# Emitting the routing and experts' stage of a retention and mixture-of-experts kernel by a model of the engines

## The chip, the cores and the metric

The kernel runs on one core of one Trainium2 chip. The metric is the device time of one execution in microseconds (us). A core has five engines that each work through their own list of instructions in order: TensorE (PE, matmuls), VectorE (DVE), ScalarE (ACT), GpSimd (POOL) and SyncE (SP, which here issues DMA transfers). An instruction starts when the one ahead of it on its engine has left and the semaphores that it waits for are there. So the order in which the kernel's author emits instructions decides what an engine does next, even when something further down its list could start already.

## The reference

Three steps follow each other: a retention (a decaying linear attention), a dense layer with a squared ReLU, and a mixture of eight experts in which each expert takes exactly 384 tokens. What matters here is the last one:

```python
def _moe2_ref(x, w_gate, w1, w2):          # x is 3072 x 512, E = 8, F = 1024
    cap = N // E                            # 384
    logits = x @ w_gate
    order = np.argsort(-logits.flatten())
    for idx in order:                       # the best pair first
        tok, e = int(idx) // E, int(idx) % E
        if assigned[tok] >= 0 or counts[e] >= cap:
            continue
        assigned[tok] = e
        counts[e] += 1
    for e in range(E):
        mask = assigned == e
        h = np.maximum(x[mask] @ w1[e], 0.0)
        out[mask] = h @ w2[e]
```

Matmuls must hold more than a 16-bit mantissa: each is made of three products of a high and a low part (high by high, high by low, low by high).

## The kernel before

The retention and the first layer fill the first 617 us. The stage that the change touches comes after them. It goes expert by expert, in the order in which experts become full, with these pieces:

- **Last block of the first layer** (`x_last`, L708): three matmuls for each of 16 slices f and four token groups c, emitted as the list `order`. Each finished group is copied by ACT (L712) and stored to the table `x2d` in DRAM (L714).
- **Search** (`search`, with `begin`): finds which tokens the next expert takes. Six rounds each of a count on PE (24 small matmuls, L831), a comparison of the counts on DVE (`sat`, L876), and new digits and comparisons on DVE (`cmp`, L823). Then come `TOT` (L909), a copy of it by ACT (`tots`, L911), and the slot matmuls (L923, L924), which this text calls the SLOT. After the SLOT, `begin` prepares the next search on DVE, with an expansion `EH` on ACT (L799, four pieces).
- **Index** (`index`): DVE makes the one-hot tables `ob`, `oa`, `pay` (L948 to L956); PE matmuls them (L962); `ixs` and L970 follow, and DVE ends with `idx` (L976).
- **Fetch** (`fetch`): POOL gathers the 384 token rows from `x2d` by `idx` in three indirect DMAs (L985). PE transposes them (`turn`, L1002). ACT makes the high part `gh` (L1024) and DVE the low part `gl` (L998).
- **Weights**: SP loads each slice f of an expert (512 KB, `eraw`, L1050) into four buffers. ACT makes the high part `h` (L1057) and DVE the low part `l` (L1066).
- **Expert** (`mlp`): for each of eight slices f, 12 matmuls into a PSUM bank (`eh_unit`, L1085; the bank alternates between 2 and 3). ACT takes the ReLU's high part `hh` (L1088) and DVE the low part `hl` (L1094), which reads the bank. Two slices later nine matmuls go into the output banks (`ey_unit`, L1106). At an expert's end `yo` is copied by ACT (L1110) and scattered by POOL (L1112).

The order comes from a weave. PE's main work is a list of units with a cost each. The sides (searches, indexes, weights, fetches) are generators that yield due times, written out by hand as tables:

```python
    SY=(4300, 3500, 2900, 450, 2600, 1200),
    IY=(600, 4600, 800),
    FE=(6500, 2800, 600),
```

`Weave.unit` adds the cost of a unit to a clock and steps each side whose time has come. What a side emits between two yields goes out in one piece on whichever engines it uses. The high and low parts of weights are emitted by `prep`, tied to places in the expert's units, in the fetch and in `fill`. Until the first tokens of expert 0 are there, PE runs 40 matmuls of ones (L1172), 28 of them as units and 4 after each of three groups of transposes.

## Time and profile before

| | us |
|---|---|
| median of three runs | 1043.21 (1043.13 to 1046.05) |
| the profiled execution | 1043.38 |
| its span, from the first to the last instruction | 1041.5 |
| PE busy | 989.6 (95%) |
| DVE busy | 714.3 (69%) |
| ACT busy | 452.8 (43%) |
| POOL busy | 77.7 (7%) |
| mean granted share of TensorE's clock | 0.991 |

The span is 1.9 us shorter than the profiled execution, and that execution is 0.2 us above the median. A busy share is a mean over the whole kernel; a stretch, or the waits of one engine, tells where time is lost. A row of a timeline gives the start and the duration of an instruction (or of several alike, with xN); in brackets stands how long its engine had been idle before, and what ended that. Matmuls overlap, so their starts tell the pace better than their durations.

### The profile page before, as it was taken

Reading aid. Unit: us, or ns where it says so; the run is one execution under the profiler, and the core shown is the slowest. Engines: PE = TensorE matmul, PEld = TensorE weight load, DVE = VectorE, ACT = ScalarE, POOL = GpSimd, SP = SyncE. Lnnn points to the kernel's source line nnn. Section 1 sums busy time; section 2 is a strip of 40 time slices with the busy share of each in tenths; the row PEclk is TensorE's granted clock in tenths of the full one; section 3 lists DMA queues with packets and bytes.
Section 4 is the critical chain, followed back from the end, with each engine's and each line's share of the span. In section 5 each row is a group of like instructions: output and inputs, shape, how many; then the busy total and the mean of one; then the engine's idle time right before and its main releaser. Section 6 shows DMA issues by size and latency. Waiting matters only on the chain.

```text
span 1041.5 us, 18741 instructions
## 1 busy us (share of the span) xinstructions
PE 989.6 (95%) x7356; PEld 861.5 (83%) x7356; DVE 714.3 (69%) x1778; ACT 452.8 (43%) x887; POOL 77.7 (7%) x100
## 2 busy tenths in 40 slices
PE   6899999999999999999999999799898889999997
PEld 5789998789899999899888777678787778788996
DVE  4799994587887787887763524666876768765531
ACT  2467665444344444344434551413434343533531
POOL 3200002000000000000000000011111020220211
PEclk9999999999999999999999999999999999999999
DMA  8533344332212120312130000513252433525620
GB/s 280 183 110 141 121 162 146 121 101 68 93 39 84 29 93 24 98 33 91 22 104 30 1 1 2 183 53 126 96 173 76 148 122 112 172 90 174 192 81 30
DMA packets 35031, 104.30 MB, mean 100 GB/s; under 512 B 4736, under 2 KB 5376, under 8 KB 34944
## 3 DMA queue, kind: packets, MB, share of 16 engines
q1 hardware_dynamic: 30384, 89.49, 26.6%
q0 software_dynamic: 3840, 12.59, 3.5%
q8 instruction: 57, 0.93, 0.4%
q10 hardware_dynamic: 720, 1.05, 0.3%
q14 instruction: 30, 0.25, 0.1%
HBM read 90.52 MB, written 12.58 MB: 99 GB/s over the span
## 4 chain that ended last, share of the span: by engine, by line
PE 68%; DVE 15%; issue 7%; DMA 5%; ACT 3%; POOL 2%; SPq 0%; POOLq 0%; DVEq 0%; ACTq 0%
PE b L419 22%; PE b L452 17%; PE b L1106 7%; PE b L1085 7%; DMA big<-x2d,idx 3%; PE b L708 2%; PE b L353 2%; PE b L326 2%; PE b L363 2%; PE b L831 2%; DVE raw L265 1%; POOL big L985 1%; DVE l L1066 1%; DVE raw L253 1%; DVE rl L442 1%
## 5 line engine op out<-in xcount | busy, mean ns | idle before, releaser
L475 DVE SCALAR_TENSOR_TENSOR scr<-tmp,wg 128x512 bf16<-128x512 f32 x288 | 198.0, 687 | 8.7 <-ACT tmp L462 3.8
L419 PE MATMUL b<-xh,l 128*128 128x256 f32 (+1 forms) x640 | 188.3, 294 | 3.4 <-DVE l L269 3.4
L419 PE MATMUL b<-xh,h 128*128 128x256 f32 (+1 forms) x640 | 188.8, 295 | 0.8 <-ACT xh L373 0.8
L419 PE MATMUL b<-xl,h 128*128 128x256 f32 (+1 forms) x640 | 188.1, 294 | 0.3 <-DVE xl L374 0.3
L426 ACT ACTIVATE r<-b 128x256 f32<-128x256 f32 x160 | 61.2, 383 | 192.6 <-PE b L419 184.3
L419 PEld LDWEIGHTS b<-xh,h 128*128 128x128 f32 x640 | 122.1, 191 | 11.0 <-ACT xh L373 1.3
L452 PE MATMUL b<-h,rh 128*128 128x512 f32 x320 | 129.3, 404 | 0.0
L419 PEld LDWEIGHTS b<-xl,h 128*128 128x128 f32 x640 | 122.0, 191 | 7.9 <-DVE xl L374 0.5
L419 PEld LDWEIGHTS b<-xh,l 128*128 128x128 f32 x640 | 122.1, 191 | 6.5 <-DVE l L269 3.8
L452 PE MATMUL b<-l,rh 128*128 128x512 f32 x320 | 126.5, 395 | 0.0
L452 PE MATMUL b<-h,rl 128*128 128x512 f32 x320 | 125.6, 392 | 0.8 <-DVE rl L442 0.8
L442 DVE TENSOR_TENSOR rl<-r,rh 128x256 fp32r<-128x256 f32 x160 | 68.5, 429 | 45.4 <-ACT rh L435 45.3
L1085 PE MATMUL b<-gh,h 128*128 128x384 f32 x256 | 91.0, 356 | 8.4 <-DVE hl L1094 8.4
L1066 DVE TENSOR_TENSOR l<-eraw,h 128x1024 fp32r<-128x1024 f32 x64 | 77.9, 1219 | 23.4 <-ACT h L1057 22.8
L1085 PE MATMUL b<-gh,l 128*128 128x384 f32 x256 | 86.7, 339 | 0.0
L1085 PE MATMUL b<-gl,h 128*128 128x384 f32 x256 | 86.5, 338 | 0.0
L1106 PE MATMUL b<-h,hl 128*128 128x512 f32 x192 | 76.8, 400 | 4.0 <-DVE hl L1094 4.0
L434 ACT ACTIVATE r<-r 128x256 f32<-128x256 f32 (+1 forms) x176 | 77.0, 438 | 5.6
L1106 PE MATMUL b<-h,hh 128*128 128x512 f32 x192 | 79.1, 412 | 0.0
L1106 PE MATMUL b<-l,hh 128*128 128x512 f32 x192 | 76.0, 396 | 0.0
L1088 ACT ACTIVATE hh<-b 128x384 fp32r<-128x384 f32 x64 | 31.3, 488 | 102.7 <-PE b L1085 96.4
L452 PEld LDWEIGHTS b<-h,rl 128*128 128x128 f32 x320 | 60.4, 189 | 15.2 <-DVE rl L442 1.5
(235 smaller groups left out, 1754.9 us busy)
## 6 DMA issues: line engine op xcount, KB each, us to landing
eraw<-in_w_dram SPq DMA_DIRECT2D x64, 512.0 KB, 3.6
q<-in_qkv_dram SPq DMA_DIRECT2D x36, 512.0 KB, 4.3
raw<-in_w_dram SPq DMA_DIRECT2D x32, 512.0 KB, 4.3
x2d<-tmp SPq DMA_DIRECT2D x20, 256.0 KB, 2.0
qdec<-in_dec_dram SPq DMA_DIRECT2D x18, 256.0 KB, 2.8
wg<-in_wgT_dram SPq DMA_DIRECT2D x4, 512.0 KB
x2d<-tmp ACTq DMA_DIRECT2D x3, 256.0 KB
first0h<-in_qkv_dram SPq DMA_DIRECT2D x2, 256.0 KB, 4.7
```

The source lines that it names most:

```text
L326: PE.matmul(ps[s][:, p * 128:(p + 1) * 128], kT[ss, p, :], qT[ss, p, :], start=(p == 0), stop=True, skip_group_check=True)
L353: PE.matmul(py[ss, p * 128:(p + 1) * 128], vt[:, p, ss], am[:, s, p], start=(p == 0), stop=(c == 0), skip_group_check=True)
L419: PE.matmul(ph, a[:, ks], b[..., kc, :], start=(kc == 0 and n == 0), stop=(kc == KC - 1 and n == 2))
L426: ACT.activation(r, ph, AF.Relu)
L434: ACT.activation(r, r, AF.Square)
L442: DVE.tensor_tensor(rl, r, rh.bitcast(F32), op=OP.subtract)
L452: PE.matmul(X2[blk][t], a[:, ts], b, start=(f == 0 and i == 0), stop=(f == NF - 1 and i == 2))
L475: DVE.scalar_tensor_tensor(scr, x, 1.0, WG[e], op0=OP.mult, op1=OP.mult, accum_out=of[:, e:e + 1])
L1066: DVE.tensor_tensor(lo, raw, hi.bitcast(F32), op=OP.subtract)
L1085: PE.matmul(PH[0], a[:, ks], b[:, kc, :], start=(kc == 0 and n == 0), stop=(kc == KC - 1 and n == 2))
L1088: ACT.activation(hh, PH[0], AF.Relu)
L1106: PE.matmul(Y[i, t], a[:, ts], b, start=(f == 0 and j == 0), stop=(f == NF2 - 1 and j == 2))
```

## The change

The weave of the last stage is replaced by a planner. Each generator now yields, ahead of each small group of instructions, the engine, a duration in ns, the names of the results that the group needs and the name of the one that it gives. `Plan` keeps one clock for each engine. Over and over it picks the stream whose next group could begin first by this model (plus a small bias for a stream), and lets that stream emit. The tables `SY`, `IY`, `FE`, `FZ` and `BG` are gone. Index and search are cut into finer groups. Weights go part by part, as three streams of their own: loads, high parts, low parts. The copies of the last block, the parts `hh`/`hl` and `gh`/`gl`, and the outputs become streams of their own that begin when their input is there by the model. No operation of the computation is added or taken away; of the matmuls of ones 30 are left.

```diff
+class Plan:
+    def begin(self, r):
+        eng, ns, needs, gives, lat, keep = r
+        if any(d not in self.T for d in needs):
+            return None
+        return max([self.clk[eng]] + [self.T[d] + keep for d in needs])
+
+    def run(self):
+        while self.streams:
+            best = None
+            for s in list(self.streams):
...
+                t = self.begin(s[1])
+                if t is not None and (best is None or t + s[2] < best[0]):
+                    best = (t + s[2], t, s)
...
+            _, t, s = best
+            eng, ns, _, gives, lat, _ = s[1]
+            self.clk[eng] = t + ns
+            if gives is not None:
+                self.T[gives] = t + ns + lat
...
+            self.advance(s)
+
+LAT = {"PE": 190.0, "ACT": 50.0, "DVE": 50.0, "POOL": 2600.0, "Q": 2500.0}
...
-    SY=(4300, 3500, 2900, 450, 2600, 1200),
-    IY=(600, 4600, 800),
...
+    KEEP=600.0,
...
-            ACT.dma_start(x2d[row:row + 128, ns], u[:, ns])
+    def x_row(c, half):
+        yield act(620 if half is None else 410, ("x", NF - 1, c, half), gives=("u", c, half))
...
-        yield SY[4]
-
+        yield pe(100, ("stb", i), *(() if last else (("ca", i),)), gives=("tot", i), keep=KEEP)
         tot = bank(6)
         PE.matmul(tot[:, 0:128], stb, ones_b, start=True, stop=True)
+        yield act(290, ("tot", i), gives=("tots", i))
...
         for t in range(GT):
+            yield op("POOL", 950 if t else 1760, ("idx", i), "x2d", gives=("xg", i, t))
...
+                yield pe(340, *(("xg", i, t) for t in range(GT)), need, gives=("T", i, kc), keep=KEEP)
...
+    def e_load():
+        for n in range(E * NF2):
...
+            yield op("Q", 1600, ("ei", i), *((("lo", n - 4),) if n > 3 else ()), gives=("raw", n))
...
+    def e_high():
...
+            yield act(1060, ("raw", n), old, gives=("hi", n))
...
+    def e_low():
...
+            yield dve(1220, ("hi", n), gives=("lo", n))
...
-    def eh_out(i, f):
-        hh, ph = HH[i, f]
-        hl = ff.tile([128, CAP], F32R, name="hl", bufs=3)
+    def eh_out(i, f, ph):
+        yield act(500, ("ph", i, f), gives=("hh", i, f))
+        hh = FF[0].tile([128, CAP], F32R, name="hh", bufs=3)
+        ACT.activation(hh, ph, AF.Relu)
+        yield dve(560, ("hh", i, f), gives=("hl", i, f))
...
+    def mains():
...
+                        yield pe(525, *needs, gives=("ph", i, f) if kc == KC - 1 else None)
+                        eh_unit(i, f, kc)
+                    plan.add(eh_out(i, f, PH[0]), -200)
...
-    for _ in range(28):
-        wv.unit(220, lambda: ones(1))
```

**Place 1: ACT, at the end of the first search** (last block of the first layer; `b_7119` and `b_7105` are the bank of `TOT`, `h_7114` and `h_7143` the first weight part). Before:

```order
L1057 ACTIVATE h_7114<-eraw 128x1024
L911 ACTIVATE tots<-b_7119 128x128
L712 ACTIVATE tmp<-b_6670,sb 128x512
L714 DMA x2d<-tmp 128x512
L1057 ACTIVATE h_7167<-eraw 128x1024
```

After:

```order
L986 ACTIVATE tots<-b_7105 128x128
L1127 ACTIVATE h_7143<-eraw 128x1024
L779 ACTIVATE tmp<-b_6670,sb 128x512
L781 DMA x2d<-tmp 128x512
L1127 ACTIVATE h_7166<-eraw 128x1024
```

The copy `tots` has moved from behind the first weight part to ahead of it.

**Place 2: DVE, behind the SLOT of the fourth search** (`hl` is the low part of a slice; `b_8982` and `b_8993` are the bank of slice f=1 of expert 2, counted from 0, and `b_8960` that of f=0). Before:

```order
L823 TENSOR_TENSOR cmp<-d,jt 128x1512
L952 TENSOR_TENSOR oa<-lowp,c_6307 128x384
L955 TENSOR_SCALAR pay<-oa,c_6307 128x24x16
L956 TENSOR_TENSOR pay<-oa,c_6307 128x24x16
L1066 TENSOR_TENSOR l_8976<-eraw,h_8975 128x1024
L1094 SCALAR_TENSOR_TENSOR hl<-b_8982,hh 128x384
```

After:

```order
L892 TENSOR_TENSOR cmp<-d,jt 128x1512
L1017 SCALAR_TENSOR_TENSOR sl<-s_8927 128x24
L1020 TENSOR_SCALAR lowp<-sl 128x24
L1021 TENSOR_SCALAR sl<-sl 128x24
L1024 TENSOR_TENSOR ob<-sl,c_6307 128x576
L1162 SCALAR_TENSOR_TENSOR hl<-b_8960,hh 128x384
L1028 TENSOR_TENSOR oa<-lowp,c_6307 128x384
L1032 TENSOR_SCALAR pay<-oa,c_6307 128x24x16
L1033 TENSOR_TENSOR pay<-oa,c_6307 128x24x16
L1162 SCALAR_TENSOR_TENSOR hl<-b_8993,hh 128x384
```

The first `hl` now stands ahead of `oa` and `pay`, the second right behind them, and no weight part stands between.

**Place 3: PE, around the same SLOT** (L1085 writes the bank of slice f=1 of expert 2; L1174 writes the output bank `b_8390` of expert 1, from its last two slices). Before:

```order
L1085 MATMUL b_8982<-gh,h_8722 128x384
L1085 MATMUL b_8982<-gl,h_8722 128x384
L1085 MATMUL b_8982<-gh,l_8723 128x384
L923 LDWEIGHTS strict
L923 MATMUL b_8986<-stb_6325,strict 128x48
L924 LDWEIGHTS tots
L924 MATMUL b_8986<-strict,tots 128x48
```

After:

```order
L1174 MATMUL b_8390<-h_8237,hl 128x512
L998 LDWEIGHTS strict
L998 MATMUL b_8914<-stb_6325,strict 128x48
L999 LDWEIGHTS tots
L999 MATMUL b_8914<-strict,tots 128x48
L1174 MATMUL b_8390<-h_8326,hh 128x512
```

The SLOT has moved from between the slices of the next expert back into the output matmuls of the current one. Behind it there now stand 15 output matmuls and 24 matmuls of slices before slice f=2 wants the bank that f=0 used; before, 21 matmuls of slices and 9 output matmuls stood between it and the first matmul of f=3, which wants the bank of f=1.

## Rows read from the trace of the kernel before

**Rows 1.** Four stretches: length, busy us (instructions) of PE, PEld, DVE, ACT, POOL; PEclk, DMA.

```profile
617.00:678.60 61.60, 55.72 (x432) 44.99 (x431) 32.81 (x115) 18.21 (x26) 0.00 (x0) 0.97 0.24 84
678.60:691.80 13.20, 11.80 (x124) 6.96 (x120) 6.19 (x25) 1.67 (x4) 3.18 (x3) 1.00 0.26 72
691.80:966.60 274.80, 252.34 (x2054) 215.63 (x2053) 193.91 (x602) 106.31 (x170) 39.28 (x52) 0.99 0.38 124
966.60:1035.00 68.40, 68.18 (x349) 61.53 (x347) 26.22 (x33) 26.05 (x40) 8.11 (x15) 1.00 0.30 101
```

**Rows 2.** What PE waited for, 617 to 1042 us: total us, times, longest.

```profile
PE b L1085 <- DVE hl L1094: 8.4, 3, 3.5
PE b L962 <- DVE pay L956: 4.9, 4, 1.6
PE b L1002 <- DMA big<-x2d,idx: 4.8, 8, 1.4
PE b L923 <- ACT tots L911: 4.1, 1, 4.1
PE b L1106 <- DVE hl L1094: 4.0, 4, 2.0
PE b L909 <- DVE sat L904: 1.4, 1, 1.4
```

**Rows 3.** Timeline at the first SLOT: start, us, engine, line, operation [idle before].

```profile
659.82 1.06 ACT L1057 ACTIVATE h<-eraw 128x1024 fp32r<-128x1024 f32 x1 [7.89 <-DMA eraw<-in_w_dram]
660.79 0.26 ACT L911 ACTIVATE tots<-b 128x128 bf16<-128x128 f32 x1
661.10 0.20 PE L923 MATMUL b<-stb,strict 128*128 128x48 bf16 x1 [4.15 <-ACT tots L911]
```

**Rows 4.** The three stretches of the stage with a lower granted clock, as in rows 1.

```profile
661.20:664.40 3.20, 3.20 (x10) 2.54 (x10) 2.79 (x11) 1.17 (x2) 0.00 (x0) 0.56 0.62 252
797.00:801.00 4.00, 4.00 (x36) 3.39 (x35) 1.49 (x4) 0.91 (x2) 0.00 (x0) 0.57 0.72 219
831.00:835.50 4.50, 4.50 (x16) 3.11 (x15) 0.00 (x0) 1.38 (x4) 2.15 (x4) 0.62 0.17 62
```

**Rows 5.** Timeline of PE and DVE behind the SLOT of 787 us.

```profile
787.15 0.43 PE L1085 MATMUL b<-gh,h 128*128 128x384 f32 x1
787.76 0.20 DVE L926 SCALAR_TENSOR_TENSOR s<-b,stb 128x48 f32<-128x48 f32 x1
790.92 0.39 PE L1106 MATMUL b<-h,hh 128*128 128x512 f32 x1
792.77 0.40 PE L1106 MATMUL b<-h,hl 128*128 128x512 f32 x1
793.65 0.55 DVE L952 TENSOR_TENSOR oa<-lowp,c 128x384 f16<-128x384 int32 x1
794.47 0.55 DVE L956 TENSOR_TENSOR pay<-oa,c 128x384 f16<-128x384 f16 x1
794.94 1.22 DVE L1066 TENSOR_TENSOR l<-eraw,h 128x1024 fp32r<-128x1024 f32 x1
796.07 0.55 DVE L1094 SCALAR_TENSOR_TENSOR hl<-b,hh 128x384 fp32r<-128x384 f32 x1
796.68 0.44 PE L1085 MATMUL b<-gh,h 128*128 128x384 f32 x1 [3.52 <-DVE hl L1094]
```

**Rows 6.** Timeline of two gathers: `idx`, POOL's third gather, the transpose that waited.

```profile
804.06 0.18 DVE L976 TENSOR_REDUCE idx<-rm 128x3 int32<-128x24 f32 x1
807.80 0.95 POOL L985 DMA_INDIRECT big<-x2d,idx  x1 [0.30 <-issue]
811.56 0.33 PE L1002 MATMUL b<-ident,big 128*128 128x128 f32 x1 [0.72 <-DMA big<-x2d,idx]
...
932.25 0.18 DVE L976 TENSOR_REDUCE idx<-rm 128x3 int32<-128x24 f32 x1
935.93 1.64 POOL L985 DMA_INDIRECT big<-x2d,idx  x1 [0.30 <-issue]
942.47 0.33 PE L1002 MATMUL b<-ident,big 128*128 128x128 f32 x1 [0.79 <-DMA big<-x2d,idx]
```

## What the change does to the time

> **What bounds the kernel now.** I read the views in this order: the stretches of the last stage, then the waits of PE, then the timeline at the longest waits. PE is the bound: in the four stretches from 617 to 1035 us it is busy for all but 29.9 us [rows 1]. Of that, 5.9 us lie before 678.6 (last block and first search), 1.4 between 678.6 and 691.8 (the wait for the first tokens, mostly covered by matmuls of ones), 22.5 while searches run beside experts 0 to 5, and 0.2 behind 966.6, where no search is left. So the end runs at PE's own pace, and nothing is to be had there. DVE, busy 194 of 275 us in the third stretch, is no bound by its total; what counts is how its list is ordered.
>
> The waits name the culprits [rows 2]. 12.4 us (8.4 + 4.0) are for `hl`; 4.9 for `pay`; 4.8 for gathered tokens; 4.1 for `tots`; 1.4 ahead of `TOT`, listed under `sat`. Two timelines show why. At the first SLOT, ACT holds `tots` behind a weight part whose DMA had not landed: ACT idles 7.89 us, then works on the weight from 659.82, and only at 660.79 copies `tots`, so PE stands 4.15 us [rows 3]. At 787 us DVE goes from the SLOT's result (787.76) through the next search's start and the whole index to the end of `pay` (795.02), then through a weight's low part, and `hl` ends at 796.62; PE, which needs its bank, had stood 3.52 us [rows 5]. The granted clock fell to half three times in the stage [rows 4]. The first two falls stand right behind these two waits.
>
> **The change part by part.** The arithmetic stays; only the order moves. Removing a wait is worth its length as long as nothing else is late then. All sums start from the profiled execution, 1043.4 us; it lies 0.2 above the median and 1.9 above its span.
>
> *First SLOT.* `tots` now stands ahead of the weight on ACT, so it waits for `TOT` alone and takes 0.26 us [rows 3]; PE has six matmuls of the last block between `TOT` and SLOT. Gone: 4.15 us. The clock behind it stood at 0.56 for 3.2 us, so 0.44 x 3.2 = 1.4 us more. What is late next is the chain behind the last block: copy, store, gather, transposes. It hangs on the block's end, so it moves up with it. Sum 5.5 us.
>
> *Low parts `hl`.* Each is a stream of its own with a bias of -200 ns. Price the round of rows 5 anew. From the SLOT's result to the start of `oa` DVE takes 793.65 - 787.76 = 5.9 us; `hl` of f=0 (0.55) now follows there, ending 6.5 to 7.1 us behind the SLOT (the result itself stood 0.6 behind, with an `hl` ahead of it). PE's pace: 21 slice matmuls from 787.15 to 790.92, 0.18 each; output matmuls 0.23 each (eight steps to 792.77) [rows 5]. In the new order 15 x 0.23 + 24 x 0.18 = 7.8 us of PE work lie between SLOT and the matmul that needs that bank. Margin 0.7 to 1.3 us, where 3.5 were missing. The next `hl` has `oa` and `pay` ahead, 1.4 us, and is done near 9; PE wants it behind nine more slice matmuls, a count and the index, after 11. So all 12.4 us go.
>
> *`pay`, `TOT`.* The index matmuls now follow the next search's first count. In the same round `pay` ends near 8.5 us behind the SLOT, and PE gets there at 7.8 + 9 x 0.18 = 9.4 plus the count: margin over 1 us. `TOT` moves to where its inputs are due by the planner's figures plus 0.6 us. Taken: 4.9 + 1.4 = 6.3 us.
>
> *Clock.* The falls at 797 and 831 us cost 0.43 x 4.0 and 0.38 x 4.5, 1.7 us each [rows 4]. If waits of 2 us and more go, so do these: 3.4 us.
>
> *Gathers.* Not removed. The planner puts the transposes 50 + 1760 + 2 x 950 + 2600 + 600 ns = 6.9 us behind `idx`. In one gather the tokens came 7.3 us behind the end of `idx` (804.24 to 811.56), in another 10.0 (932.43 to 942.47) [rows 6]. At 7.3 each transposition of experts 1 to 7 waits about 0.4 us, 3 us in all; now it is 4.8 less the 1.4 of the first tokens, 3.4 [rows 1, 2]. Taken as unchanged; the ends are -3.4 (all waits gone) and 3.1 us more in a round. From the end of POOL's third issue to the transpose these rows have 2.8 us (808.75 to 811.56) and 4.9 us (937.57 to 942.47) [rows 6]. The Trainium skill ("DMA: Bandwidth & Descriptors", section "Anatomy of one DMA — SWDGE (gpsimd) path") gives a DMA issued by GpSimd a fixed 2.0 us plus its bytes over 436 GB/s; an estimate from that page for the 256 KB of one gather is 2.6 us. By the page the planner's place is late enough and the sum would be 31.0 instead of 27.6 us; the first row is 0.2 us above it, the second 2.3 us.
>
> *Weights part by part.* DVE and ACT run the same parts. They lie beside PE work; the cover is four buffers, and PE has had no wait for a weight among its six largest [rows 2]. Nothing is taken. In exchange, a weight's low part (1.22 us, rows 5) can stand ahead of a search step.
>
> *Fewer matmuls of ones, two more counts ahead of expert 0.* The wait for the first tokens has its own chain, 13.2 us [rows 1]. I take zero, with 1 us either way.
>
> Sum of gains: 5.5 + 12.4 + 6.3 + 3.4 = 27.6 us. The new order is fixed by rounded durations and has margins of about 1 us in a round, and DVE is loaded at 70%. A part that comes late by more than its margin stops PE again. The bounds for new waits are 0 and 10 us (half of what `hl`, `pay` and `TOT` cost now, 18.7); I take 4, some 0.6 us in each of the seven rounds from the first search's end on, the size of the smaller waits now [rows 6]. Net gain 23.6: 1043.4 - 23.6 = 1019.8, or **1020 us**. With all gains, no new wait and no wait for gathers it is 1043.4 - 27.6 - 3.4 = 1012; with 10 us of new waits 1026.
>
> **The rivals.**
> *The waits come back.* DVE's list is still one list, and a step that the planner thought ready (a low part whose `h` is late, a search step whose count PE has not reached) holds the `hl` behind it. For it speaks that DVE now has weights between search steps; against it the margins above. If two thirds of 18.7 us return and so do both clock falls, the gain is 27.6 - 12.5 - 3.4 = 11.7: 1032 us.
> *The gathers are hidden.* If the tokens of each expert are there 6.9 us behind `idx`, the transposes of experts 1 to 7 wait for nothing and the 3.4 us go too: 1019.8 - 3.4 = 1016.4. For it speaks the wait of only 0.72 us at 811.56, against it the 10.0 us of the other gather [rows 6]. This is what the page of the Trainium skill named above would have.
> *The clock falls ahead of expert 0.* Ten matmuls of ones fewer stand around the first transposes; with forty the trace has a clock of 1.00 in this stretch [rows 1]. The price is one more fall, 1.4 to 1.7 us [rows 4]: 1021.4 us.
> *The planner's order does not change PE's waits.* If most of them are set by the DMA and by the length of the search, other engines are named but the sum stays: 1043 us. Against it: rows 3 and 5 show orders, not durations, that end the waits.
> *Slower: the gathers run late in every round.* Place: transposes of experts 1 to 6, now placed by the planner 6.9 us behind `idx`. Weight loads are now spread over the round, and they share the DMA engines with the gather. If each gather takes the 10.0 us of the second one in rows 6, PE stands 3.1 us six times and the clock falls behind each (1.6 us, the mean of rows 4): 28.2 us. Today's 3.4 us of gather waits are replaced, so the time is 1019.8 + 28.2 - 3.4 = 1044.6, still no change that can be told. At 10.5 us, half a microsecond worse than that row, it is 1019.8 + 6 x 5.2 - 3.4 = 1047.6, slower; the point is 10.3 us. Against it: of eight such waits none was over 1.4 us [rows 2].
>
> **How the numbers follow.** A measurement here can tell 0.3%, some 3 us. Forecast (1012 to 1026, taken at 1020): 0.54. Gathers hidden (1016.4): 0.10. Clock fall ahead of expert 0 (1021.4): 0.05. Waits come back (1027 to 1037, taken at 1032): 0.17. Unchanged within 0.3%: 0.07. Slower through gathers (1047.6): 0.07. The range from 1011 to 1036 leaves out the last two and the edges. Faster: 0.54 + 0.10 + 0.05 + 0.17 = 0.86; same 0.07; slower 0.07.
>
> **What would show it.** In the profile after: the wait of the SLOT for `tots` gone and the last block ended some 6 us earlier; PE's wait for `hl` under 3 us; one or no stretch at half clock behind 700 us; waits for gathered tokens at 2 to 5 us in sum; the last two experts as long as before. It would be wrong if PE's wait for `hl`, `cmp` or `sat` is over 10 us again, if waits for gathers pass 1.5 us each, or if a wait for `h` or `l` shows up on PE.

## The result and the profile after

| | before | after |
|---|---|---|
| median, us | 1044.04 | 1008.17 (1005.84 to 1009.08) |
| ratio, with its 95% interval | | 0.965 (0.963 to 0.967) |
| the profiled execution, us | 1043.4 | 1008.7 |
| its span, us | 1041.5 | 1006.9 |
| last block of the first layer | 60.5 | 54.1 |
| from there to the first slice matmul (the front) | 13.2 | 15.2 |
| experts, first slice matmul to last output matmul | 343.0 | 312.3 |

The change makes the kernel some 36 us faster. The forecast was 1020 us with a range down to 1011, so the direction and most of the mechanism were right; the gain was 12 us more than forecast, and the time lies 3 us below the range.

The four stretches of the kernel after answer to [rows 1]. Columns as there; they are the last block, the front, experts 0 to 5, and experts 6 and 7.

```profile
618.50:672.70 54.20, 53.59 (x453) 44.00 (x452) 30.67 (x117) 16.36 (x25) 0.00 (x0) 1.00 0.22 76
672.70:687.85 15.15, 12.07 (x136) 7.22 (x133) 9.46 (x34) 4.25 (x6) 4.26 (x3) 0.89 0.44 131
687.85:932.00 244.15, 243.33 (x2004) 212.67 (x2005) 207.04 (x601) 119.31 (x181) 39.81 (x52) 1.00 0.49 157
932.00:1000.20 68.20, 68.18 (x349) 61.58 (x347) 13.66 (x22) 15.06 (x28) 9.97 (x16) 1.00 0.11 36
```

Read the third row against the third of [rows 1]. There PE was idle 22.5 of 274.8 us; now it is idle 0.8 of 244.2. Its granted clock was 0.99 and is 1.00 (a clock of 1.00 is the 2.4 GHz level, and a mean below it means that the lower level, 1.2 GHz, was granted in part). The front is the one place that got worse: 0.89, and 2 us longer. The waits of PE from 617 to 1010 us, in total us, times and longest, answer to [rows 2]:

```profile
PE b L1077 <- DMA big<-x2d,idx: 2.9, 2, 2.5
PE b L1154 <- DVE gl L1073: 0.8, 1, 0.8
PE b L771 <- ACT tmp L779: 0.6, 1, 0.6
PE b L1154 <- ACT gh L1071: 0.2, 1, 0.2
```

Nothing of [rows 2] is left except gathered tokens, and those 2.9 us are expert 0's, in the front. No wait for `hl`, `pay`, `tots` or `sat` is listed. What is new is 1.0 us for `gl` and `gh` at the start of expert 0; the wait for `tmp` was there before (0.6 us).

The round behind one SLOT (767.74 us) shows how. It is the counterpart of [rows 5]: timelines of PE and of DVE, with start, duration, engine, line and operation.

```profile
767.74 0.20 PE L998 MATMUL b<-stb,strict 128*128 128x48 bf16 x1
...
775.50 0.33 PE L1154 MATMUL b<-gh,h 128*128 128x384 f32 x1
...
777.07 0.94 PE L900 MATMUL b<-cmp,EH 128*128 128x63 bf16 x24
777.93 0.76 PE L1038 MATMUL b<-ob,pay 128*32 128x24 f16 x24
```

```profile
768.00 0.21 DVE L1002 SCALAR_TENSOR_TENSOR s<-b,stb 128x48 f32<-128x48 f32 x1 [0.15 <-PE b L999]
...
774.22 0.55 DVE L1162 SCALAR_TENSOR_TENSOR hl<-b,hh 128x384 fp32r<-128x384 f32 x1
774.68 0.55 DVE L1028 TENSOR_TENSOR oa<-lowp,c 128x384 f16<-128x384 int32 x1
...
775.50 0.56 DVE L1033 TENSOR_TENSOR pay<-oa,c 128x384 f16<-128x384 f16 x1
776.28 0.56 DVE L1162 SCALAR_TENSOR_TENSOR hl<-b,hh 128x384 fp32r<-128x384 f32 x1 [0.23 <-ACT hh L1159]
```

The first `hl` ends 7.0 us behind the SLOT and `pay` 8.3; the prediction had 6.5 to 7.1 and 8.5. Between the SLOT and 775.50 stand 15 output and 24 slice matmuls, as laid out there, so PE comes 0.7 us behind that `hl`, where in [rows 5] it stood for 3.52.

### The profile page after: what moved, and what is told of

The parts are those of the page before. It is cut to its first block, busy times and chain, and to the rows that moved or that the text cites. A ratio compares the mean times of both kernels' runs of the same rounds, so it can differ in the third digit from the quotient of the medians.

```text
span 1006.9 us, 18668 instructions
## 1 busy us (share of the span) xinstructions
PE 980.3 (97%) x7346; PEld 859.4 (85%) x7346; DVE 715.8 (71%) x1778; ACT 455.8 (45%) x887; POOL 80.8 (8%) x100
## 4 chain that ended last, share of the span: by engine, by line
PE 86%; DVE 4%; issue 4%; DMA 2%; ACT 1%; POOL 1%; SPq 0%; POOLq 0%; DVEq 0%; ACTq 0%
PE b L482 25%; PE b L515 20%; PE b L1154 12%; PE b L1174 12%; PE b L771 5%; PE b L900 3%; PE b L416 2%; PE b L389 2%; PE b L426 2%; PE b L1077 1%; PE b L422 1%; DMA qdec0h<-in_dec_dram 1%; DVE raw L328 1%; PE b L755 1%; DVE l L332 1%
## 5 line engine op out<-in xcount | busy, mean ns | idle before, releaser
L505 DVE TENSOR_TENSOR rl<-r,rh 128x256 fp32r<-128x256 f32 x160 | 68.2, 427 | 45.9 <-ACT rh L498 45.8
L1127 ACT ACTIVATE h<-eraw 128x1024 fp32r<-128x1024 f32 x64 | 67.4, 1057 | 45.7 <-DMA eraw<-in_w_dram 42.6
L1174 PE MATMUL b<-h,hh 128*128 128x512 f32 x192 | 78.6, 409 | 0.0
L1174 PE MATMUL b<-h,hl 128*128 128x512 f32 x192 | 75.6, 394 | 0.0
L1162 DVE SCALAR_TENSOR_TENSOR hl<-b,hh 128x384 fp32r<-128x384 f32 x64 | 35.5, 555 | 56.3 <-ACT hh L1159 55.5
L1174 PE MATMUL b<-l,hh 128*128 128x512 f32 x192 | 75.4, 393 | 0.0
```

What stands on the lines that cost most here:

```text
L505: DVE.tensor_tensor(rl, r, rh.bitcast(F32), op=OP.subtract)
L1127: ACT.activation(hi, ERAW[n], AF.Copy)
L1162: DVE.scalar_tensor_tensor(hl, ph, 0.0, hh.bitcast(F32), op0=OP.max, op1=OP.subtract)
L1174: PE.matmul(Y[i, t], a[:, ts], b, start=(f == 0 and j == 0), stop=(f == NF2 - 1 and j == 2))
```

## Experiments

Each ratio is to the kernel before on the same chip in the same group of runs. The kernel after had 0.965 (0.963 to 0.967) in its first group and 0.968 (0.966 to 0.970), at 1008.3 us, in a later one (r1_after), so ratios of different groups compare to about 0.003. The names of the kernels stand in the text, lines of code under them.

### The first SLOT alone (e1_tots)

The kernel before, with one thing changed: no weight part goes onto ACT until `tots` has.

```diff
-                if n >= 2 * NF and n % 4 == 0 and (0, f) in ERAW:
+                if n >= 2 * NF and n % 4 == 0 and (0, f) in ERAW and TURN:
...
         ACT.activation(tots, tot[:, 0:128], AF.Copy)
+        TURN.append(i)
```

> The kernel before with one thing changed: no weight part is put on ACT until the copy tots of the first search is on its list. Theory of order (each long wait comes from where one instruction stands on ACT or DVE): the 4.15 us wait of the SLOT and the half clock behind it go, 5.5 us, so 1038.5 us against 1044.0 (median of four runs), and the waits for hl stay at 12 us. Rival (a wait that goes is taken up by the chain behind the last block): the last block ends 5 us earlier but expert 0 begins at most 2 us earlier, 1042 us.

1036.2 us, a ratio of 0.995 (0.993 to 0.997): 5.5 us at that group's 1041.9. The timelines of ACT and PE at the first SLOT, against [rows 3]:

```profile
654.52 0.28 ACT L911 ACTIVATE tots<-b 128x128 bf16<-128x128 f32 x1 [3.60 <-PE b L909]
...
658.87 1.06 ACT L1058 ACTIVATE h<-eraw 128x1024 fp32r<-128x1024 f32 x1 [1.38 <-DMA eraw<-in_w_dram]
```

```profile
655.77 0.20 PE L924 MATMUL b<-stb,strict 128*128 128x48 bf16 x1
```

The weight part now comes 4 us behind `tots` instead of ahead of it. The 5.5 us of the prediction's first term are shown, without any planner.

### One due time in the old tables (e2_tots_iy)

The same, and the index starts 2.9 us later by the old weave.

```diff
-    IY=(600, 4600, 800),
+    IY=(3500, 4600, 800),
```

> As e1_tots, and in the hand-written table the first due time of the index side is 3500 ns instead of 600, so that DVE gets the low parts hl of the slices beside it ahead of ob, oa and pay. Theory of order: a good half of the 12.4 us of waits for hl goes, and some of the 1.7 us for a fall of the clock, 8 us less than e1_tots, 1031 us; the gathers begin 2.9 us later in each round, which the transposes' place (hand-written, too) follows. Rival (one number cannot do it, the planner is needed, since what is late next are pay, idx and the gathers): the waits for hl fall, those for pay and for gathered tokens rise by as much, 1036 to 1040 us.

1027.9 us, 0.986 (0.984 to 0.989), 8 to 9 us less than e1_tots. PE's waits for `pay` (5.4 us in e1_tots) are off its list, those for `hl` fell from 12.2 to 10.0 us. So two edits of the old order give some 14 us. The time is the theory's (8 us), but not the way to it: I had put it on a good half of the waits for `hl`, and by PE's list most of it came from `pay`. The one number tried here leaves 10 us of waits for `hl`.

### `hl` behind `pay` again (e4_hl_pay)

The kernel after, with the first `hl` of experts 1 to 5 held behind `pay` of the next index, as DVE had them in [rows 5].

```diff
-        yield dve(560, ("hh", i, f), gives=("hl", i, f))
+        late = (("pay", i + 1),) if f == 0 and 1 <= i <= 5 else ()
+        yield dve(560, ("hh", i, f), *late, gives=("hl", i, f))
```

> The changed kernel, with the low part hl of the first slice of experts 1 to 5 put behind pay on DVE, as it stood before the change; the planner knows it and orders the rest around it. Theory of order: hl ends 1.4 us later, at 7.9 to 8.5 us behind the SLOT, where PE wants the bank at 7.8: waits for hl of 0.3 to 0.7 us in five rounds, 2 to 3 us in all, 1010.5 us. Rival (the early SLOT alone does it): no wait for hl, 1008 us.

1024.2 us, 0.984 (0.982 to 0.987): 16 us more, and 11 in the profiled execution. I had put 2 to 3. In expert 1 the planner, finding no slice matmul to place, put the next search's count there instead. Timeline of DVE and PE in that round:

```profile
732.62 0.56 DVE L1163 SCALAR_TENSOR_TENSOR hl<-b,hh 128x384 fp32r<-128x384 f32 x1 [0.65 <-ACT hh L1159]
...
734.81 0.95 DVE L892 TENSOR_TENSOR cmp<-d,jt 128x1512 bf16<-128x1512 bf16 x1
735.81 1.13 PE L900 MATMUL b<-cmp,EH 128*128 128x63 bf16 x18 [3.75 <-DVE cmp L892]
...
738.28 0.55 DVE L1163 SCALAR_TENSOR_TENSOR hl<-b,hh 128x384 fp32r<-128x384 f32 x1
```

The wait that was hl's is now called `cmp`. PE stands 3.75 us, the expert takes 49.2 us instead of 41, and its mean clock is 0.90. In the profiled execution PE waits 3.8 us for `cmp`, 3.5 us more for gathers than in the kernel after, and only 1.3 for `hl`. So the place of `hl` matters, but since the planner lays other rounds around it, this run does not give the price of `hl` alone.

### What keeps new waits away (e5_keep0, e12_keep0_gather, e16_keep0_paced, e6_dve07)

KEEP lays each count, TOT, SLOT, index matmul and transpose 0.6 us behind the moment at which its inputs are due. First without it:

```diff
-    KEEP=600.0,
+    KEEP=0.0,
```

> The kernel after, with the planner's constant KEEP at 0 instead of 600 ns: counts, TOT, SLOT, index matmuls and transposes are placed on PE 0.6 us nearer to the moment at which their inputs are due by the model. In the trace of the kernel after, the inputs of the 30 counts behind 690 us were there 0.65 us or more ahead of PE, those of SLOT, TOT and the index 0.96 us or more. Theory, the model's durations are right and KEEP is only spare: the smallest margins fall to about 0.05 us, no wait for cmp, sat, pay or tots comes back above 1 us in sum, and only the transposes, which had 0.06 to 1.2 us, wait, some 1 to 2 us in all: 1007 to 1011 us, under 0.3% from the kernel after. Rival, the margin is what kept the new waits of my forecast away: of some 80 such groups a third wait 0.3 us, 8 us, and the clock falls once or twice, so 1017 us or more.

1034.6 us, 0.993 (0.991 to 0.995): 26 us more, most of the gain. My theory fell. The rival's time (1017 us or more) came true, but not its waits: 14.4 us were for gathered tokens, and only 4 us for all else, with a clock of 0.983. So I put the transposes back where they had been (delay behind a gather 3.2 instead of 2.6 us):

> KEEP at 0 as in e5_keep0, but with the delay behind a gather at 3.2 instead of 2.6 us, so that the transposes stay where the kernel after has them and counts, SLOT and index matmuls come 0.6 us nearer to their inputs. e5_keep0 took 26 us more than the kernel after; its PE waited 14.4 us for gathered tokens and some 4 us for all else. Theory, the gathers alone make this loss, by their waits and the clock that falls with them: 1008 to 1014 us, waits for gathers under 5 us, for all else under 5 us. Rival, the lost margin of the search and index groups makes the rounds irregular and the gathers late with it: 1025 us or more.

1030.3 us, 0.990 (0.987 to 0.992), so the place of the transposes was not the cause. The two views below suggest what was; they are of an execution of 1037.8 us, the longest of its five. First the stretch of expert 2, columns as in [rows 1]:

```profile
779.10:836.40 57.30, 49.48 (x453) 42.41 (x452) 47.91 (x162) 22.25 (x34) 7.65 (x10) 0.88 0.33 102
```

In the kernel after this expert takes 40.8 us, with 354 matmuls and 107 DVE instructions; here it has 453 and 162, and ten counts instead of six. Without KEEP's eight groups of 0.6 us a search is some 5 us shorter, gets ahead of its expert, and the planner puts more than one search beside an expert. DVE works 47.9 us there, and PE waits for `cmp` (4.4 us in all), `l`, `hl` and `pay`. Second, the timeline of POOL at the gather of expert 4:

```profile
837.50 1.82 POOL L1182 DMA_INDIRECT out_dram<-yo,idx  x1 [0.22 <-DVE cmp L892]
839.63 0.99 POOL L1063 DMA_INDIRECT big<-x2d,idx  x1 [0.30 <-PE b L1154]
```

and the same in the kernel after:

```profile
813.28 1.38 POOL L1182 DMA_INDIRECT out_dram<-yo,idx  x1 [0.34 <-ACT yo L1179]
823.35 1.22 POOL L1063 DMA_INDIRECT big<-x2d,idx  x1 [8.69 <-issue]
```

Its `idx` had been there for 41 us (798.25), so the gather stands right behind a scatter instead of 8.7 us later. The next run keeps KEEP at 0, but gives the search its pace back, by a result of the SLOT that is due 4.8 us later:

```diff
-        yield pe(150, ("tots", i), gives=("slot", i), keep=KEEP)
+        yield pe(150, ("tots", i), gives=("slot", i), lat=190 + 4800, keep=KEEP)
```

> The kernel of e12_keep0_gather, with the result of each SLOT due 4.8 us later in the model, about what KEEP takes from one search in the kernel after (eight groups of 0.6 us). Counts, SLOT and index matmuls still stand right where their inputs are due, but a search no longer gets ahead of its expert: by the model idx of experts 2 to 6 lies 11 to 18 us behind the SLOT again and 11 to 18 us behind the outputs of the expert before the last, while in e12_keep0_gather idx of experts 3 and 4 was ready before them, and POOL issued the gather 0.30 us behind a scatter. Theory, the 22 us that KEEP is worth are the pace of the search: 1006 to 1014 us, waits for cmp, pay and the like of at most 4 us in sum. Rival, they are the margin between an input and PE: 1022 us or more.

1010.8 us, 0.971 (0.969 to 0.973): 19.5 of the 22 us are back. The stretch of expert 2, and PE's waits of 0.4 us or more from 617 to 1030 us:

```profile
770.00:812.20 42.20, 41.19 (x355) 35.73 (x354) 34.67 (x107) 18.07 (x28) 8.79 (x8) 1.00 0.41 136
```

```profile
PE b L1077 <- DMA big<-x2d,idx: 5.9, 6, 1.9
PE b L771 <- ACT tmp L779: 0.6, 1, 0.6
PE b L900 <- ACT EH L866: 0.4, 1, 0.4
```

The expert has 355 matmuls and 107 DVE instructions again, and no wait for `cmp` or `pay` is listed, though counts came as little as 0.15 us behind their inputs (in the kernel after 0.65). So most of what KEEP buys is the pace: one search to an expert. The rest, 3 to 6 us by the ratios of the kernel after, is not told apart; PE waits 3.0 us more for gathers here than in the kernel after.

The last run of this group planned with DVE's durations at 0.7 of what they are:

> The kernel after, planned with all of DVE's durations at 0.7 of what they are. A search step's comparisons are then due 0.7 us too early, an index's pay 0.8 us and its gather 0.9 us. Theory, the durations have to be right to within the 0.6 us of KEEP: waits for cmp and pay of 0.1 to 0.3 us in many rounds, 5 us in sum, and waits for gathers between those of the kernel after (2.9 us) and of e7_gather_early (16.5 us with the transposes 1.6 us early), with clock falls behind them: 1015 to 1028 us. Rival, the order of the groups decides and not the durations: 1005 to 1011 us.

1031.7 us, 0.992 (0.989 to 0.995). PE waits 8.3 us for gathers, 7.0 for `cmp` in nine places, 3.7 for `pay`. It, too, has the searches ahead of their experts: ten, eight and nine counts beside experts 0 to 2, where the kernel after has six. The stretch of expert 0:

```profile
690.90:744.70 53.80, 49.01 (x475) 41.64 (x476) 47.69 (x141) 27.51 (x41) 5.15 (x5) 0.94 0.40 133
```

So it doesn't tell wrong durations from wrong pace. It shows that the gain hangs on DVE's durations being about right.

### Gathers 1.6 us early, and with the loads held off (e7_gather_early, e13_early_fenced)

```diff
-LAT = {"PE": 190.0, "ACT": 50.0, "DVE": 50.0, "POOL": 2600.0, "Q": 2500.0}
+LAT = {"PE": 190.0, "ACT": 50.0, "DVE": 50.0, "POOL": 1000.0, "Q": 2500.0}
```

> The kernel after, with the planner's delay behind each gather at 1.0 us instead of 2.6: transposes are placed 1.6 us earlier. In the kernel after, the data of the six gathers of experts 1 to 6 landed 0.60, 0.56, 1.16, 0.06, 0.71 and 0.67 us before PE came to the transposes. Theory, the place of the transposes alone decides whether PE waits for a gather: waits of 1.0, 1.0, 0.4, 1.5, 0.9 and 0.9 us in those rounds, 5.8 us, and about 1 us more in front of expert 0, no clock fall behind a wait this short: 1013 to 1016 us. Rival, gathers come when the rest of the round lets them and the waits stay where they are: 1007 to 1010 us.

1029.1 us, 0.988 (0.986 to 0.989): 21 us more, where my theory, the place alone, had 6. The waits for gathers are 16.5 us, and the tokens themselves came later. The second run adds this behind the gather's third issue, so that SP's next load can't start before the tokens are there (and tells the planner):

```diff
+        if 0 < i < E - 1:
+            SP.dma_start(held[i:i + 1, :], xg[0:1, GT - 1, 0:16])
```

> The kernel of e7_gather_early, with a DMA of 64 bytes on SP that reads the last gathered tokens of experts 1 to 6, so that a weight load behind it can't start while the gather runs. In e7_gather_early a load was issued 1.9, 3.4 and 3.4 us behind the start of the gathers of experts 3, 4 and 5, and their last tokens came to PE 4.3, 5.0 and 4.5 us behind POOL's third issue; in the kernel after, with loads at 0.5 and 5.2 us or more, 2.4 to 3.3 us. Theory, the 512 KB load beside the gather delays it: 2.5 to 3.3 us in those rounds, waits for gathers 16.5 to about 10 us in sum, rounds 4 us shorter where they were 47, and 1014 to 1021 us. Rival, gathers were late from POOL's side or by their place: 4 to 5 us stay, 1026 us or more.

1023.1 us, 0.982 (0.980 to 0.985), between the theory's 1014 to 1021 and the rival's 1026. The gather of expert 5 is a clean pair, with POOL's three issues equally long and a first load 0.8 us behind the gather's start in both. Timelines of POOL, SP and PE in e7_gather_early, and the stretch of its round:

```profile
877.35 1.53 POOL L1063 DMA_INDIRECT big<-x2d,idx  x1 [8.58 <-PE b L900]
...
880.62 0.95 POOL L1063 DMA_INDIRECT big<-x2d,idx  x1 [0.30 <-issue]
```

```profile
878.13 2.94 SPq L1119 DMA_DIRECT2D eraw<-in_w_dram  x2
```

```profile
886.02 1.12 PE L1077 MATMUL b<-ident,big 128*128 128x128 f32 x4 [1.35 <-DMA big<-x2d,idx]
```

```profile
866.50:913.40 46.90, 43.93 (x357) 37.62 (x356) 35.33 (x107) 19.96 (x31) 7.21 (x10) 0.93 0.42 137
```

and in e13_early_fenced:

```profile
872.95 1.53 POOL L1064 DMA_INDIRECT big<-x2d,idx  x1 [8.58 <-PE b L901]
...
876.23 0.95 POOL L1064 DMA_INDIRECT big<-x2d,idx  x1 [0.30 <-issue]
```

```profile
873.74 0.33 SPq L1123 DMA_DIRECT2D eraw<-in_w_dram  x1
879.82 0.28 SPq L1067 DMA_DIRECT2D held<-big  x1
```

```profile
879.84 0.65 PE L1081 MATMUL b<-ident,big 128*128 128x128 f32 x4 [0.39 <-DMA big<-x2d,idx]
```

```profile
862.10:905.20 43.10, 41.76 (x357) 35.84 (x356) 35.27 (x107) 19.86 (x31) 7.25 (x10) 1.00 0.46 150
```

From the end of POOL's third issue to the last tokens it is 4.5 us with a second 512 KB load issued 3.4 us behind the gather's start, and 2.7 us without. The round falls from 46.9 to 43.1 us and its clock goes back to 1.00. For expert 4 the delay fell only from 5.0 to 3.7 us. For expert 3 it fell from 4.3 to 3.7, but there the load 1.9 us behind the gather's start stood ahead of the 64-byte DMA in SP's list and was not held. PE still waits 12.2 us in sum. So holding the loads, with the planner told of it, gives 6 of the 21 us. That the rest is the early place and the falls of the clock behind it is what is left over, not tested by itself.

### The front (e3_head, e8_head_late, e9_loads_only, b1_loads_held, r1_after, e15_front_fenced, b2_front_only, b3_all_fenced)

In the kernel after SP issues the last two weight loads of expert 0 beside the last store and the first gather. Four runs moved them, or so I thought:

```diff
+            held = (("xg", 0, GT - 1),) if n in (6, 7) else ()
-            yield op("Q", 1600, ("ei", i), *((("lo", n - 4),) if n > 3 else ()), gives=("raw", n))
+            yield op("Q", 1600, ("ei", i), *((("lo", n - 4),) if n > 3 else ()), *held, gives=("raw", n))
...
-        plan.T["x2d"] = plan.T["u", 3, 1] + 2200
+        plan.T["x2d"] = plan.T["u", 3, 1] + 3700
```

(The lines on `x2d` in e3_head and e8_head_late only; e8_head_late with a delay behind a gather of 3.6 us.)

> The changed kernel, with the loads of weight parts 6 and 7 of expert 0 held until the first gather is issued by the planner's clock, and the planner's time of the table x2d set 1.5 us later (3700 ns instead of 2200 behind the last copy), so that more matmuls of ones stand before the transposes. Theory (the 2.0 us that the stretch between last block and expert 0 has become longer come from two weight loads that share the DMA with the last store and the gather, and from the fall of the clock behind a wait of 2.5 us): the stretch goes from 15.2 to 13.0 us, the clock stays, 1006 us against 1008.2. Rival (the chain of store, issue and gather has its own length and the loads do not matter): 15 us as now, 1008 us.

1009.8 us, 0.969 (0.967 to 0.971), the rival's time: the front is 13.6 us long at a clock of 1.00, but the experts take 4.2 us more.

> The kernel of e3_head (the last two weight loads of expert 0 held until its gather is through, and the gather due 1.5 us later in the model), with the delay behind each gather at 3.6 instead of 2.6 us. In e3_head the stretch from the last block to the first slice matmul was 13.6 us, 1.6 less than in the kernel after, but the experts took 4.2 us more, of which PE waited 3.1 for gathered tokens of experts 1, 2, 5 and 6. Theory, those waits are a margin of under 1.3 us that is missing: they go, the front stays under 14 us, and the run is 3 us below e3_head, some 1.5 us below the kernel after: a ratio to before of 0.964. Rival, the 4.2 us come from another order of the rounds: ratio 0.968 to 0.969 again.

1008.6 us, 0.968 (0.967 to 0.970), with 3.6 us of waits for gathers where the theory had none: the rival.

> The kernel after, with the last two weight loads of expert 0 held until its gather is through, and nothing else; the matmuls of ones stay as they are. In the kernel after the two loads were issued at 672.8 and 676.0 us, beside the last store and the gather, PE waited 2.5 us for the first tokens, and the clock stood at half behind that for 3.4 us. Theory, the loads slow store and gather: the stretch from the last block to the first slice matmul falls from 15.2 to 13.6 to 14.2 us, with a wait for tokens near 1.5 us. Rival, the gather's own chain sets the wait and the smaller number of matmuls of ones the clock: the stretch stays at 15 us with a fall of the clock in it.

1006.7 us, 0.967 (0.965 to 0.969), with a front of 13.8 us.

> The kernel of e9_loads_only again (the kernel after, with the last two weight loads of expert 0 held until its gather is through). Theory, the loads beside store and gather are what made the clock fall there: a front of 13.8 us without a fall, and 1 to 2 us less than the kernel after in the same group. Rival, the fall in the kernel after was of that one execution: both take the same time within 0.1%.

1008.6 us, 0.969 (0.967 to 0.971).

> The kernel after once more, to have it on the same chip as the others of this group: a ratio to before of 0.963 to 0.967, 1004 to 1009 us, and the two stretches as before: 15 us from the last block to the first slice matmul, 312 us for the experts.

1008.3 us, 0.968 (0.966 to 0.970), so b1_loads_held changes nothing. The edit is a line in the planner, and it only moves the loads further down SP's list. SP had nothing else to do and waits for nothing of the gather, so in all these runs it issued them at the same times, the first some 5.1 and the second 1.9 to 2.0 us ahead of POOL's gather. An order is not a wait. The same kernel had a front of 13.8 us without a fall of the clock in e9_loads_only and, on another chip, of 14.7 with one in b1_loads_held, so that fall comes and goes between executions, and is worth 1 us. The next run holds the loads by a DMA of 64 bytes that reads the gathered tokens, as above, for expert 0:

> The kernel after, with a DMA of 64 bytes on SP that reads the last gathered tokens of expert 0, ahead of the last two weight loads of expert 0. In e9_loads_only and b1_loads_held those loads stood further down SP's list, but nothing held them, and their times were the same (2.0 us ahead of the gather); this one holds them. Theory, they slow the last store or the gather: POOL's first issue 4.3 instead of 5.2 us behind the last block, PE's wait for the first tokens under 1.7 instead of 2.5 us, a front of 13 to 14 us instead of 15, and 1 to 2 us less than the kernel after. Rival, store and gather take as long without the loads: wait 2.4 to 2.6 us, front 13.8 to 15 us with the clock as it happens to fall, same time within 0.1%.

1010.6 us, 0.971 (0.969 to 0.972). The front was 11.0 us, less than the theory had, but the experts took 318.9: the planner had been told of the wait and had laid other rounds, with 4.6 us of waits for gathers. Without that line the lists of the other engines stay as in e9_loads_only:

> The kernel of e15_front_fenced without the line that tells the planner of the wait, so that PE, DVE, ACT and POOL work through the same lists as in e9_loads_only, and only SP has the 64-byte DMA more. e15_front_fenced had a front of 11.0 us instead of 15 and a first gather that began 3.1 instead of 5.3 us behind the last block, but its experts took 319 us, 7 more than in the kernel after, with 4.6 us of waits for gathers. Theory, the front is the loads' doing and the 7 us came from the plan that had been laid anew around other due times: front 11 to 12 us, experts 312 to 314 us, 1004.5 to 1006 us, a ratio to before 0.003 below that of the kernel after in the group before (0.965). Rival, the loads of the rounds shift against the gathers by the 4 us that the front is shorter, whatever the lists: experts 316 us or more, no gain.

1005.3 us, 0.963 (0.961 to 0.965), the lowest ratio of all. The kernel after has no run in this group; against its 0.965 and 0.968 it is 2 to 5 us, hardly more than what groups differ by. The front is clear: 11.0 us here and in e15_front_fenced. Stretches of the front and of experts 0 to 5:

```profile
672.50:683.50 11.00, 10.56 (x140) 6.52 (x136) 9.15 (x33) 2.20 (x4) 3.11 (x3) 1.00 0.29 86
683.50:929.40 245.90, 243.42 (x2003) 212.64 (x2004) 206.73 (x602) 120.94 (x183) 39.90 (x52) 1.00 0.51 160
```

POOL and SP there, and then in the kernel after:

```profile
675.65 1.21 POOL L1064 DMA_INDIRECT big<-x2d,idx  x1 [109.87 <-DMA x2d<-tmp]
```

```profile
682.08 0.31 SPq L1067 DMA_DIRECT2D held<-big  x1
682.63 7.63 SPq L1123 DMA_DIRECT2D eraw<-in_w_dram  x4
```

```profile
677.96 2.01 POOL L1063 DMA_INDIRECT big<-x2d,idx  x1 [112.02 <-DVE cmp L892]
```

```profile
672.81 3.50 SPq L1119 DMA_DIRECT2D eraw<-in_w_dram  x2
```

The first gather begins 3.1 instead of 5.3 us behind the last block, and its first issue takes 1.21 instead of 2.01 us. Most of the first comes from the last store: with a load issued 0.4 us ahead of it, it landed 3.8 us behind its issue (r1_after, b1_loads_held), without the loads 1.7 us (here and in e15_front_fenced). So the two loads cost the front 3 to 4 us: 13.8 us at a clock of 1.00 in e9_loads_only, and 15.2 with a fall of it in the kernel after, against 11.0. Half of it is given back in the experts (314.2 instead of 312.3 us). The last run puts the 64 bytes behind the gathers of experts 1 to 6 as well:

> The same with the 64-byte DMA behind the gathers of experts 1 to 6 too. Theory, as in e13_early_fenced no last tokens come later than 3.8 us behind POOL's third issue, in the rounds with a load 2 to 5 us behind the gather's start 0.5 to 1.5 us earlier than without; where PE had a margin it gains nothing by that: within 1 us of b2_front_only, or as much below it as that run waits for gathers in its rounds. Rival, the loads held back make a weight's part late, and PE waits for h or l: 2 us or more above it.

1010.4 us, 0.969 (0.967 to 0.971), 5 us more than b2_front_only. Waits for gathers are down to 0.2 us, but PE waits 5.6 us for `gl`, 1.2 of them in the front. Timelines of ACT and DVE at one of these waits:

```profile
754.50 1.06 ACT L1131 ACTIVATE h<-eraw 128x1024 fp32r<-128x1024 f32 x1 [4.43 <-DMA eraw<-in_w_dram]
755.46 1.03 ACT L1074 ACTIVATE gh<-b,cT 128x384 fp32r<-128x384 f32 x2
```

```profile
756.06 1.14 DVE L1076 SCALAR_TENSOR_TENSOR gl<-b,cT,gh 128x384 fp32r<-128x384 f32 x2 [3.64 <-ACT gh L1074]
```

The held load comes late, ACT stands at its `h`, and `gh` and `gl` stand behind that, just as `tots` did in [rows 3]. It is the rival, by one engine's list more: in this plan, where PE had a margin at the gathers, holding the loads costs.

## Why the prediction was right and wrong

In the two profiled executions the span fell by 34.6 us. The forecast was 23.6, and its own end with no new wait and no wait for gathers was a fall of 31.0. Term by term:

- **First SLOT, 5.5 us: right.** e1_tots alone gave 5.5. The last block fell by 6.3, which holds a wait for `pay` and one for `EH` of the same stretch.
- **`hl`, 12.4 us: right by PE's list,** where no such wait is left, down to the margin of 0.7 us in the round shown above. Undoing the order (e4_hl_pay) costs 11 to 16 us, but mostly by other waits, so no run prices `hl` alone.
- **`pay` and `TOT`, 6.3 us: right.** Neither is on PE's list.
- **Clock, 3.4 us: right** for the two falls of [rows 4] behind 700 us: the third and fourth stretch stand at 1.00.
- **New waits, 4 us with ends of 0 and 10: too large, 1.0 at most** (`gl` and `gh` at the start of expert 0; 0.9 us for `cmp`, not in the sum, went). I reasoned that lists fixed by rounded durations, with margins of about 1 us, must lose some 0.6 us in each of seven rounds. The runs show that margins down to 0.15 us bring no wait for `cmp` or `pay` back (e16_keep0_paced), and that what matters more is whether search and expert keep the same pace. The kernel after does; e5_keep0, e12_keep0_gather and e6_dve07 don't, and lose 22 to 26 us. In time they are near my rival "the waits come back" (1032 us), but PE waits there for gathers and `cmp`, hardly for `hl`.
- **Gathers, taken as unchanged: wrong, 3.4 us better.** The transposes of experts 1 to 6 wait for nothing; the end of -3.4 us came true. PE comes to them 7.1 to 9.0 us behind `idx`, not 6.9 as in the planner's figures, so part of this is slack that I had not forecast. I had read the two late gathers of [rows 6] as the gather's own length. The pair of expert 5 shows that a load beside it can make 1.8 us of it. The Trainium skill ("DMA: Bandwidth & Descriptors", section "Anatomy of one DMA — SWDGE (gpsimd) path") has a fixed 2.0 us plus the bytes over the bandwidth, for which the estimate was 2.6 us. The trace agrees for expert 7 in e7_gather_early, beside whose gather no load runs (2.6 us from the end of POOL's third issue to the transposes), and nearly so in the pair's second run (2.7 us), but not where the second load is issued (4.5 us).
- **Weights part by part, taken as nothing: wrong in the front.** I named four buffers as the cover for PE. What I didn't cost is the loads' own traffic at new times: beside the last store and the first gather they cost 3 to 4 us (b2_front_only).
- **Matmuls of ones and counts, zero with 1 us either way: wrong together with that.** The front took 2.0 us more. The rival in which the clock falls ahead of expert 0 took place (0.89), but the ten matmuls of ones alone do not decide on the fall: the same kernel has it in one execution and not in another.
- **PE's own pace: not in the sum, 5.6 us. This is the step that failed.** The prediction has "Removing a wait is worth its length", and takes the two counts ahead of expert 0 at zero. New waits and gathers lie inside its own ends, so they don't bring the time below them; this term does. In [rows 1] PE is busy 252.3 + 68.2 us from the first slice matmul to the last output, in the kernel after 243.3 + 68.2, 9.0 less. Of these 3.4 are the clock, 1.3 the two counts (48 matmuls at 0.028 us). The other 4.3 us seem to go with the waits themselves. A wait is listed from the end of the last matmul, but the next one would have begun before that end: in [rows 5] a matmul begins at 792.77 and lasts 0.40 us, the next was due 0.23 us behind its start, at 793.00, and came at 796.68. That is 3.68 us late, where the list has 3.52. The stretch of expert 4 before and after:

```profile
881.70:927.70 46.00, 42.04 (x354) 35.79 (x353) 35.38 (x113) 19.01 (x30) 6.64 (x10) 1.00 0.38 125
853.30:894.20 40.90, 40.90 (x355) 35.78 (x354) 35.21 (x109) 20.08 (x31) 6.74 (x10) 1.00 0.49 155
```

About as many matmuls at the same clock; before, with four waits, PE is busy 1.1 us longer beside the 4.0 us that it is idle. Experts 6 and 7 have no wait in either kernel, and PE is busy 68.18 us in both. An estimate from the starts of the matmuls around all 21 waits of the third stretch of [rows 1], against the usual pace of the same matmuls, gives 4.9 us beyond the listed lengths, and 0.4 us in the kernel after. No run changed this alone.

New waits 4.0, gathers 3.4, PE's pace and the two counts 5.6, less 2.0 for the front: 11.0, the difference between 34.6 and 23.6. The first two lead to the 1012 us that the prediction has for no new wait and no wait for gathers; the 3.6 us below it are PE's pace and the two counts, less the front.

The slower rival was not idle talk: gathers late in every round, at 3.1 us of wait and 1.6 of clock each. In e7_gather_early three rounds of 47 us against 41 have that, 2.7 to 3.7 us of waits and 1.7 to 3.4 of clock. It needed transposes only 1.6 us earlier.

## What to carry over

Where a planner lays the lists of all engines, ask first whether its streams run at one pace: a side that gets ahead by a few us in a round crowds one round and starves the next, and cost more here (22 to 26 us) than all the small margins. A transfer has a place in time only by a real wait; a line in a list of an otherwise idle queue holds nothing. A listed wait is the least that it costs: where matmuls overlap, add some 0.2 us for each (4.9 us for 21 waits here, an estimate). When a change spreads loads over a round, price them where they pass another transfer that an engine waits for.

## What the runs showed of the hardware

- A 512 KB load beside a gather (three DMAs of 256 KB each) can delay its last tokens: 4.5 us behind POOL's third issue with a second load issued 3.4 us behind the gather's start (e7_gather_early, expert 5), 2.7 us without that load (e13_early_fenced). The size varies: with a load held back it was 3.7 us for expert 4.
- Two loads beside the last store and the first gather put off that gather by 2.2 us and came with a first issue on POOL of 2.01 instead of 1.21 us. The store landed 3.8 us behind its issue instead of 1.7 (r1_after, b2_front_only).
- The granted clock fell in the front in one execution of a kernel and not in another, on two chips, behind waits for tokens of the same 2.4 us (b1_loads_held 0.88, e9_loads_only 1.00 as means over the front).
- By the profile PE is busy until its last matmul ends, 0.40 us, though the next one begins 0.23 us behind a start [rows 5]. So a wait took some 0.2 us more than its listed length (an estimate from 21 waits of the kernel before).
